# Unread loads, products, transpositions and copies ahead of a cached-attention decode kernel

## The chip, the core and the metric

The kernel runs on one core of a Trainium2 chip. The metric is device time in microseconds (us). The core has a matrix engine (PE, whose weight loads are listed as PEld), a vector engine (DVE), a scalar engine (ACT), GpSimd (POOL) and SyncE (SP), whose queue issues nearly all transfers here, and 16 DMA engines that move data between HBM and the on-chip memory of 128 partitions.

## The reference

One decode step of a transformer block with adaptive layer norm, all in float32:

```
mod = (silu(c) @ w_mod) -> sa, ca, ga, sb, cb, gb
h = layernorm(x) * (1 + ca) + sa
q = h @ wq                                  # 8 batches, 32 heads, Dh = 128
k, v = the last 2048 of 8192 cached rows of each of 8 batches x 8 KV heads
x = x + ga * (softmax(q k^T / sqrt(128)) v) @ wo
h = layernorm(x) * (1 + cb) + sb
x = x + gb * (relu(h @ w1 + b1)**2 @ w2 + b2)
```

The part of the caches that is read is 64 MiB of K and 64 MiB of V, each float32. The cache lies as (batch, KV head, row, 128): one head is 4 MiB apart from the next, one batch 32 MiB.

## The kernel before

The kernel is one long stream of 1 to 2 MiB transfers on SP's queue into eight buffers, `slot0` to `slot7`, of 128 partitions x 16 KiB. The list `loads` fixes their order: `w_mod` for the first modulation (`modA`), two pieces of `wq`, then K and V blocks with the other weights between them, `V` five blocks behind `K` (`V_LAG`). `pump()` issues the next load whenever a slot is free, and `done()` frees a slot after its last reader. A block (`load`, L96) is one KV head of two batches: each batch is 1 MiB, contiguous in HBM, and goes to every second partition (`t[u::2, :]`).

The work ahead of the first block is short: SP issues `w_mod`, while ACT and DVE build `cT`, the transposed silu of the condition (L208 to L211, L204); PE makes the modulation from both (L220); a layer norm; and the first half of q (L266). Then a loop over 32 blocks transposes each K block on PE with a multiplication by the identity (L299), copies the result out of PSUM on ACT and DVE in turn (L300), multiplies by q (L311), and, with a softmax per KV head, multiplies V (L391). [...] Products with 32 weight columns are issued in fours, one for each quarter of the array, and overlap. The output projection and the MLP end the kernel.

The order on each engine is the order in which the code is written (`manual_schedule`); waits are generated from reads and writes of tiles. The pools `work`, `ktp` and the four PSUM pools are opened at the start; the slots lie in `consts`.

Of the kernel before, what the change touches and what calls it, by code (L numbers as in the profile page):

```python
# [8 lines left out]
F32 = mybir.dt.float32  # L9
# [5 lines left out]
SLOTS = 8  # L15
# [5 lines left out]
def tile_adaln_cached_attention_mlp(  # L21
# [14 lines left out]
    nc = tc.nc  # L36
    P = 128
    B, HKV, SK, DH = k_cache.shape
# [3 lines left out]
    W = min(4096, max(256, SK // 4))  # L42
    F = w1.shape[1]
    NJ = 2 * W // P
# [7 lines left out]
    assert (B, D, DH, REP, NJ, NQ, F) == (8, 512, 128, 4, 32, 4, 1792)  # L52

    consts = ctx.enter_context(tc.tile_pool(name="consts", bufs=1))
    work = ctx.enter_context(tc.tile_pool(name="work", bufs=2))
    ktp = ctx.enter_context(tc.tile_pool(name="ktp", bufs=6))
    ps_kt = ctx.enter_context(tc.tile_pool(name="ps_kt", bufs=2, space=bass.MemoryType.PSUM))
    ps_m = ctx.enter_context(tc.tile_pool(name="ps_m", bufs=2, space=bass.MemoryType.PSUM))
    ps_o = ctx.enter_context(tc.tile_pool(name="ps_o", bufs=2, space=bass.MemoryType.PSUM))
    ps_1 = ctx.enter_context(tc.tile_pool(name="ps_1", bufs=1, space=bass.MemoryType.PSUM))  # L60
    ctx.enter_context(tc.manual_schedule())


# [8 lines left out]
    ident = consts.tile([P, P], F32, name="ident")  # L72
# [4 lines left out]
    nc.vector.memset(eps, EPS)  # L77


    slots = [consts.tile([P, NJ * DH], F32, name=f"slot{i}") for i in range(SLOTS)]  # L80
    free = list(range(SLOTS))
    held = {}
    r_kc = "(p kc) n -> p kc n"
# [355 lines left out]
    for s in range(N + PV_LAG + 1):  # L439
        g, i = divmod(s, C)  # L440
# [55 lines left out]
    for kc in range(NQ):  # L496
        for g in range(NQ):
# [4 lines left out]
                start=False,  # L502
                stop=(kc == NQ - 1),
# [16 lines left out]
    for f in range(FC):  # L520
        for q in range(NQ):
# [4 lines left out]
                start=False,  # L526
                stop=(f == FC - 1),
# [41 lines left out]
```

## Time and profile before

| what | value |
|---|---|
| median of the runs | 405.19 us (2 runs: 405.01 to 405.38) |
| span of the profiled execution | 403.6 us |
| around the span | 1.6 us to the median |
| PE, DVE, ACT, POOL busy | 83%, 44%, 24%, 1% |
| moved by DMA | 165.25 MB, mean 409 GB/s |

The median is that of unprofiled runs; the page shows one profiled execution, and the difference of 1.6 us is what lies around its span. "Busy" of PE is pipelined time, so 83% is not a share of its peak. The DMA rows carry the weight here: how much was moved, at what rate, and how long a transfer took from its issue to its landing.

### The profile page before, as it was taken

The page shows a single profiled execution, that of the slowest core. Times are in us where ns is not written, and L with a number is a line of the kernel's source. Part 1 is how long each engine was busy: PE and PEld are TensorE (multiplying, and loading weights), DVE is VectorE, ACT ScalarE, POOL GpSimd, SP SyncE. Part 2 cuts the span into 40 slices and gives each one's busy share as a digit, 9 for nine tenths or more (in the row PEclk, how much of TensorE's full clock was granted, in tenths as well). Part 3 has the DMA queues.
Part 4 walks back from the last instruction along what each step waited for, and adds up shares of the span by engine and source line. Part 5 has one row for each costly group of instructions (what it writes and reads, how often), then busy time and mean ns, then how long its engine had stood idle before and what let it go on. Part 6 is the DMA issues. An engine that isn't in the chain of part 4 may idle for free.

```text
span 403.6 us, 6379 instructions
## 1 busy us (share of the span) xinstructions
PE 333.1 (83%) x2632; PEld 170.0 (42%) x2632; DVE 177.2 (44%) x405; ACT 94.9 (24%) x168; POOL 4.1 (1%) x12
## 2 busy tenths in 40 slices
PE   0688899898998398999998899988688999884685
PEld 0245455354544155445544454444344454331124
DVE  5223345345554235445644464446344554344222
ACT  1223244123312022222222322232122322120000
POOL 4000000000000000000000000000000000000000
PEclk9789999999999889999999999999999999969659
DMA  8999999999999999999999999999999999999970
GB/s 312 429 430 424 418 429 429 427 423 421 433 429 412 430 430 424 428 429 418 433 425 430 424 432 420 434 416 429 429 425 430 425 425 430 421 427 426 408 304 8
DMA packets 15406, 165.25 MB, mean 409 GB/s; under 512 B 2441, under 2 KB 2705, under 8 KB 4497
## 3 DMA queue, kind: packets, MB, share of 16 engines
q1 hardware_dynamic: 15168, 164.70, 96.8%
q8 instruction: 21, 0.34, 0.3%
q10 hardware_dynamic: 144, 0.13, 0.1%
q14 instruction: 9, 0.07, 0.0%
q0 software_dynamic: 64, 0.01, 0.0%
HBM read 164.77 MB, written 0.07 MB: 408 GB/s over the span
## 4 chain that ended last, share of the span: by engine, by line
DMA 64%; PE 24%; DVE 6%; ACT 4%; issue 1%; ACTq 0%; DVEq 0%; SPq 0%
DMA slot<-in_A_v_cache_dram 25%; DMA slot<-in_A_k_cache_dram 20%; DMA slot<-in_A_wo_dram 17%; PE kt_ps L299 8%; PE s_ps L311 4%; PE o_ps L391 3%; PE m_ps L266 2%; DVE kT L300 2%; ACT kT L300 2%; DMA slot<-in_w_mod_dram 2%; PE m_ps L498 1%; PE m_ps L220 1%; PE m_ps L522 1%; DVE o_sb L404 1%; PE wo_ps L428 1%
## 5 line engine op out<-in xcount | busy, mean ns | idle before, releaser
L299 PE MATMUL kt_ps<-ident,slot 128*128 128x128 f32 x1024 | 150.2, 285 | 33.1 <-DMA slot<-in_A_k_cache_dram 14.9
L299 PEld LDWEIGHTS kt_ps<-ident,slot 128*128 128x128 f32 x1024 | 110.5, 143 | 106.2 <-issue 63.0
L300 DVE COPY kT<-kt_ps 128x512 f32<-128x512 f32 x128 | 88.3, 690 | 103.9 <-PE kt_ps L299 93.3
L300 ACT COPY kT<-kt_ps 128x512 f32<-128x512 f32 x128 | 74.9, 585 | 212.7 <-PE kt_ps L299 182.4
L391 PE MATMUL o_ps<-slot,pT 128*32 128x512 f32 x512 | 65.8, 625 | 6.4 <-DMA slot<-in_A_v_cache_dram 6.4
L311 PE MATMUL s_ps<-kT,qpad 128*32 128x512 f32 x512 | 64.3, 618 | 0.0
L404 DVE SCALAR_TENSOR_TENSOR o_sb<-o_ps,diag,o_sb 128x128 f32<-128x128 f32 x96 | 33.7, 351 | 3.4
L402 DVE TENSOR_SCALAR o_sb<-o_ps,diag 128x128 f32<-128x128 f32 x32 | 11.2, 351 | 44.5 <-PE o_ps L391 44.5
L391 PEld LDWEIGHTS o_ps<-slot,pT 128*32 128x32 f32 x512 | 16.4, 111 | 31.6 <-issue 27.5
L311 PEld LDWEIGHTS s_ps<-kT,qpad 128*32 128x32 f32 x512 | 13.3, 108 | 26.7 <-issue 26.7
L220 PE MATMUL m_ps<-slot,cT 128*32 128x256 f32 (+2 forms) x96 | 7.3, 451 | 9.1 <-DMA slot<-in_w_mod_dram 9.1
L266 PE MATMUL m_ps<-slot,h1T 128*32 128x512 f32 x64 | 9.8, 766 | 2.2 <-DVE h1T L204 2.2
L325 DVE TENSOR_REDUCE mx<-ss 128x1 f32<-128x512 f32 x8 | 5.5, 686 | 13.8 <-ACT ss L323 13.8
L413 PE MATMUL m_ps<-o_sb,pick 128*32 128x512 f32 x64 | 8.4, 594 | 3.1 <-DVE o_sb L404 1.6
L371 DVE TENSOR_TENSOR pT<-m_ps,mine 128x512 f32<-128x512 f32 x16 | 10.3, 682 | 0.4 <-PE m_ps L368 0.4
L428 PE MATMUL wo_ps<-slot,oT 128*32 128x512 f32 x64 | 9.6, 675 | 1.1 <-DVE oT L418 1.1
L417 DVE STREAM_TRANSPOSE tr<-m_ps 128x512 f32<-128x512 f32 x8 | 5.7, 716 | 9.5 <-PE m_ps L413 9.5
L220 PEld LDWEIGHTS m_ps<-slot,cT 128*32 128x32 f32 x96 | 4.4, 132 | 12.2 <-DVE cT L204 9.1
L368 PE MATMUL m_ps<-ident,pr 128*128 128x128 f32 x64 | 9.2, 292 | 0.3 <-DVE pr L352 0.3
L323 ACT COPY ss<-s_ps 128x512 f32<-128x512 f32 x8 | 4.7, 587 | 18.5 <-PE s_ps L311 18.5
L368 PEld LDWEIGHTS m_ps<-ident,pr 128*128 128x128 f32 x64 | 7.9, 151 | 1.3 <-DVE pr L352 1.3
L351 ACT ACTIVATE pr<-ss,nm 128x512 f32<-128x512 f32 x8 | 6.1, 762 | 9.5 <-DVE nm L347 9.5
(103 smaller groups left out, 91.1 us busy)
## 6 DMA issues: line engine op xcount, KB each, us to landing
slot<-in_A_k_cache_dram SPq DMA_DIRECT2D x64, 1024.0 KB, 20.0
slot<-in_A_v_cache_dram SPq DMA_DIRECT2D x64, 1024.0 KB, 19.9
slot<-in_A_wq_dram SPq DMA_DIRECT2D x4, 2048.0 KB, 19.9
slot<-in_A_wo_dram SPq DMA_DIRECT2D x4, 2048.0 KB, 22.3
slot<-in_B_w_dram SPq DMA_DIRECT2D x2, 1792.0 KB, 22.3
slot<-in_w_mod_dram SPq DMA_DIRECT2D x2, 1536.0 KB, 21.5
slot<-in_B_w_dram SPq DMA_DIRECT2D x3, 1024.0 KB, 23.5
slot<-in_w_mod_dram SPq DMA_DIRECT2D x1, 2048.0 KB, 8.2
```

The lines of the kernel that those rows point to most:

```text
L220: nc.tensor.matmul(pm[32 * q : 32 * q + 32, : nq * P].rearrange("p (m n) -> p m n", m=nq), cT[:, kc, :], wv[:, :, q, :], start=(kc == 0), ...
L266: nc.tensor.matmul(pq[32 * g : 32 * g + 32, :], hT[:, kc, :], w[:, kc % 2, 512 * g : 512 * g + 512], start=(kc == 0), stop=(kc == NQ - 1),)
L299: nc.tensor.transpose(p[:, i, :], k[:, 8 * g + 4 * a + i, :], ident)
L300: (nc.vector.tensor_copy if a else nc.scalar.copy)(t[:, 4 * a : 4 * a + 4, :], p)
L311: nc.tensor.matmul(s_ps[0][32 * g : 32 * g + 32, :].rearrange("p (i r) -> p i r", i=8), qpad[:, hk, 2 * c + u, :], KTS[n, g][:, :, u::2], ...
L368: nc.tensor.transpose(pp[:, i * P : (i + 1) * P], pr[:, 4 * a + i].rearrange("p r u -> p (r u)"), ident)
L371: nc.vector.tensor_mul(PT_[hk][:, a].rearrange("p x i r -> p i x r"), pp.rearrange("p (i x r) -> p i x r", i=4, r=2 * REP), mine.rearrange ...
L391: nc.tensor.matmul(o[32 * g : 32 * g + 32].rearrange("p j d -> p (j d)"), PT_[hk][:, h, C * g + c].rearrange("p i r -> p (i r)"), v[:, j : ...
L402: nc.vector.tensor_scalar(d, o[:, 0, :], diag[:, 0:1], None, op0=ALU.mult)
L404: nc.vector.scalar_tensor_tensor(d, o[:, j, :], diag[:, j : j + 1], d, op0=ALU.mult, op1=ALU.add)
L413: nc.tensor.matmul(pp[32 * t : 32 * t + 32, :], pick[:, t, :], o.rearrange("p c d -> p (c d)"), start=True, stop=True)
L428: nc.tensor.matmul(wo_ps[32 * i : 32 * i + 32, :], oT[hk % 2][:, i, :], w[:, 4 * (hk % 2) + i, :], start=(hk == 0), stop=(hk == HKV - 1),)
```

## The change

Ahead of everything but the constants stands a block that works on four buffers of its own: `trial0` to `trial2` (32 KiB in each of 128 partitions, 4 MiB each) and `trial_big` (64 KiB, 8 MiB). It loads parts of K (and once V) into them in five layouts, runs products and transpositions on `trial2` into two PSUM tiles, and transpositions and copies of `trial1` into `trial0` on DVE, ACT and GpSimd. Nothing of it is read by the rest. The block's pools are closed at its end, and the pools of the old kernel are opened behind it, so they take the same memory: 160 KiB in each partition for the block, 128 KiB for the slots. The slots move from `consts` to a pool of their own. The rest is unchanged, 81 lines further down (L96 is L177, L123 is L204, L220 is L301).

```diff
+    with tc.tile_pool(name="trial", bufs=1) as trial, tc.tile_pool(
+        name="ps_trial", bufs=1, space=bass.MemoryType.PSUM
+    ) as ps_trial:
+        pr_ = [trial.tile([P, 64 * DH], F32, name=f"trial{i}") for i in range(3)]
+        big = trial.tile([P, 128 * DH], F32, name="trial_big")
...
+        t0 = (SK - W) * DH
...
+        hs, bs, run = SK * DH, HKV * SK * DH, 64 * DH
+        for t, q in ((pr_[0], 0), (pr_[1], 1)):
+            nc.sync.dma_start(t, dram(k_cache, t0 + q * run, [[hs, 16], [4 * run, 8], [1, run]]))
+        for t, h in ((pr_[2], 0), (pr_[0], 1)):
+            nc.sync.dma_start(t, dram(k_cache, t0 + h * hs, [[run, 32], [bs, 4], [1, run]]))
+        for t, h in ((pr_[1], 2), (pr_[2], 3)):
+            for b in (0, 2, 1, 3):
+                nc.sync.dma_start(
+                    t[32 * b : 32 * b + 32, :], dram(k_cache, t0 + h * hs + b * bs, [[run, 32], [1, run]])
+                )
+        nc.sync.dma_start(big, dram(k_cache, t0, [[2 * run, 16], [bs, 8], [1, 2 * run]]))
+        nc.sync.dma_start(pr_[0], dram(k_cache, t0, [[bs, 8], [2 * run, 16], [1, run]]))
+        nc.sync.dma_start(pr_[1], dram(v_cache, t0, [[run, 32], [hs, 4], [1, run]]))
...
+        def product(n, dims, reps, step=32, width=512):
+            for k in range(reps):
+                for g in range(4):
+                    nc.tensor.matmul(
+                        po[n][32 * g : 32 * g + 32, :width],
+                        ident[:, 32 * (k % 4) : 32 * (k % 4) + 32],
+                        view(t, step * g, dims),
+                        start=True,
+                        stop=True,
+                    )
+
+        product(0, [[1, 512]], 12)
+        product(1, [[1, 512]], 4)
+        product(0, [[128, 64], [1, 8]], 4)
+        product(1, [[128, 64], [4, 8]], 4, step=1)
+        product(0, [[4, 8], [128, 64]], 4, step=1)
+        product(1, [[1, 8], [128, 64]], 4)
+        product(0, [[128, 64], [8, 4], [1, 2]], 4, step=2)
+        product(1, [[60, 128], [1, 4]], 4)
+        product(0, [[128, 32], [1, 16]], 4)
+        product(1, [[128, 32], [2, 16]], 4, step=1)
+        product(0, [[128, 8], [2, 64]], 4, step=1)
+        product(1, [[1, 128]], 16, width=128)
+        product(0, [[4096, 2], [1, 128]], 8, width=256)
+        for k in range(8):
+            nc.tensor.transpose(po[1][:, 128 * (k % 4) : 128 * (k % 4) + 128], t[:, 128 * k : 128 * k + 128], ident)
+        for k in range(8):
+            nc.tensor.transpose(po[0][:, 128 * (k % 4) : 128 * (k % 4) + 128], view(t, k, [[32, 128]]), ident)
+        for k in range(16):
+            g = 32 * (k % 4)
+            nc.tensor.matmul(po[1][g : g + 32, :256], view(t, k, [[4, 32]]), view(t, 0, [[4096, 2], [1, 128]]), start=True, stop=True)
+        for k in range(8):
+            nc.tensor.matmul(po[0], t[:, :128], view(t, 0, [[1, 512]]), start=True, stop=True)
+        u, w = pr_[1], pr_[0]
+        for k in range(3):
+            nc.vector.transpose(u[:, 2048 * k : 2048 * k + 2048], u[:, 2048 * k : 2048 * k + 2048])
+        nc.vector.transpose(w[:, :2048], u[:, :2048])
+        nc.vector.transpose(w[:, :512], u[:, :512])
...
+        nc.vector.tensor_copy(view(w, 0, [[512, 4], [1, 512]]), view(u, 0, [[1, 4], [4, 512]]))
+        nc.scalar.copy(w[:, 2048:4096], u[:, 2048:4096])
...
+        nc.scalar.copy(po[1], u[:, 2048:2560])
+        nc.gpsimd.tensor_copy(w[:, 4096:6144], u[:, 4096:6144])
...
+    slotp = ctx.enter_context(tc.tile_pool(name="slotp", bufs=1))
+    slots = [slotp.tile([P, NJ * DH], F32, name=f"slot{i}") for i in range(SLOTS)]
```

In `dram`, a pair is [step, count] in elements, `hs` is one KV head (4 MiB), `bs` one batch (32 MiB) and `run` 32 KiB; in `view` it is [step, count] of the elements that the moving operand takes within each partition.

What SP's queue holds at its start before the change (a row is an instruction with the tile that it writes; `DMAHW0` and the like are the counters of transfers, on which it waits for one that was issued earlier):

```order
L123 DMA slot_93<-in_w_mod_dram 128x4x1024
L123 DMA slot_94<-in_A_wq_dram 128x2x2048
L123 DMA slot_95<-in_A_wq_dram 128x2x2048
L96 DMA slot_96<-in_A_k_cache_dram 64x4096 x2
L96 DMA slot_97<-in_A_k_cache_dram 64x4096 x2
```

And after it, from the fourth transfer on (`trial_81` is `trial0`, `trial_82` is `trial1`, `trial_83` is `trial2`); ahead of these rows stand three more, into the three trial buffers, without a wait:

```order
L89 DMA trial_81<-in_A_k_cache_dram 128x1x8192 [waits DMAHW1_49]
L92 DMA trial_82<-in_A_k_cache_dram 32x8192 [waits DMAHW2_49]
L92 DMA trial_82<-in_A_k_cache_dram 32x8192 x2
L92 DMA trial_82<-in_A_k_cache_dram 32x8192 [waits DMAHW0_49]
L92 DMA trial_83<-in_A_k_cache_dram 32x8192 [waits DMAHW3_49]
L92 DMA trial_83<-in_A_k_cache_dram 32x8192 x2
L92 DMA trial_83<-in_A_k_cache_dram 32x8192 [waits DMAHW4_49]
L95 DMA trial_big<-in_A_k_cache_dram 128x1x16384 [waits DMAHW5_49]
L96 DMA trial_81<-in_A_k_cache_dram 128x1x8192 [waits DMAHW6_49]
L97 DMA trial_82<-in_A_v_cache_dram 128x1x8192 [waits DMAHW7_49,DMAHW0_49]
L204 DMA slot_484<-in_w_mod_dram 128x4x1024 [waits DMAHW3_49,DMAHW2_49,DMAHW4_49,DMAHW1_49,DMAHW5_49,DVE_49,DMAHW6_49,PE_49,DMAHW7_49,Activation_49,Pool_49]
L204 DMA slot_485<-in_A_wq_dram 128x2x2048
```

The first load of the old kernel has moved behind fifteen transfers, and it waits for counters of all of them and of PE, DVE, ACT and GpSimd.

On PE, the start before the change:

```order
L220 MATMUL m_ps<-slot_93,cT 32x256 [waits DMAHW1_49,DVE_49]
L220 MATMUL m_ps<-slot_93,cT 32x256 x15
L232 MATMUL m_ps<-xsum,sel 128x1 [waits DVE_49]
L242 MATMUL m_ps<-ssq,sel 128x1 [waits PE_49,Activation_49]
L266 MATMUL m_ps<-slot_94,h1T 32x512 [waits DMAHW2_49,DVE_49]
```

And after it, the first two and the last rows of the block, the latter with what follows:

```order
L108 MATMUL ps_trial_100<-trial_83,ident 32x512 [waits DMAHW3_49,DMAHW2_49,DMAHW4_49,DMAHW1_49,Pool_49]
L108 MATMUL ps_trial_100<-trial_83,ident 32x512 x47
L108 MATMUL ps_trial_101<-trial_83,ident 32x512 x16
L108 MATMUL ps_trial_100<-trial_83,ident 32x512 x16
L108 MATMUL ps_trial_101<-trial_83,ident 32x512 x16
```

```order
L108 MATMUL ps_trial_101<-trial_83,ident 32x128 x64
L108 MATMUL ps_trial_100<-trial_83,ident 32x256 x32
L130 MATMUL ps_trial_101<-ident,trial_83 128x128 x8
L132 MATMUL ps_trial_100<-ident,trial_83 128x128 x8
L135 MATMUL ps_trial_101<-trial_83 32x256 x16
L137 MATMUL ps_trial_100<-trial_83 128x512 x8
L301 MATMUL m_ps<-slot_484,cT 32x256 [waits DMAHW0_49,DMAHW5_49,DVE_49,DMAHW6_49,PE_49,DMAHW7_49,Activation_49,Pool_49]
L301 MATMUL m_ps<-slot_484,cT 32x256 x15
```

The block's 344 matmuls stand ahead of the modulation; their only wait is that of the first one, for the four transfers of L92 into `trial2`.

More of the change, by code (lines that the diff above doesn't have):

```diff
@@ L54, in tile_adaln_cached_attention_mlp @@
     consts = ctx.enter_context(tc.tile_pool(name="consts", bufs=1))
[L55 to L60, printed above, removed]
     ctx.enter_context(tc.manual_schedule())
@@ L77, in tile_adaln_cached_attention_mlp, with dram, view @@
     nc.vector.memset(eps, EPS)
-    slots = [consts.tile([P, NJ * DH], F32, name=f"slot{i}") for i in range(SLOTS)]
+    with tc.tile_pool(name="trial", bufs=1) as trial, tc.tile_pool(
[3 more added lines that the diff above has]
+        big = trial.tile([P, 128 * DH], F32, name="trial_big")
+        kx = k_cache.rearrange("b h s d -> (b h) (s d)")
+        t0 = (SK - W) * DH
+        def dram(src, offset, dims):
+            return bass.AP(tensor=src.tensor, offset=src.offset + offset, ap=dims)
+        hs, bs, run = SK * DH, HKV * SK * DH, 64 * DH
[11 more added lines that the diff above has]
+        nc.sync.dma_start(pr_[1], dram(v_cache, t0, [[run, 32], [hs, 4], [1, run]]))
+        po = [ps_trial.tile([P, 512], F32, name=f"ps_trial{i}") for i in range(2)]
+        t = pr_[2]
+        def view(t, offset, dims):
+            return bass.AP(tensor=t.tensor, offset=t.offset + offset, ap=[t.ap[0]] + dims)
+        def product(n, dims, reps, step=32, width=512):
[35 more added lines that the diff above has]
+        nc.vector.transpose(w[:, :512], u[:, :512])
+        nc.vector.transpose(view(w, 0, [[8, 64], [512, 4], [1, 8]]), view(u, 0, [[128, 64], [1, 32]]))
+        nc.vector.transpose(view(w, 0, [[2, 64], [128, 32]]), view(u, 0, [[128, 64], [1, 32]]))
+        nc.vector.tensor_copy(view(w, 0, [[512, 4], [1, 512]]), view(u, 0, [[1, 4], [4, 512]]))
+        nc.scalar.copy(w[:, 2048:4096], u[:, 2048:4096])
+        nc.scalar.copy(view(w, 2048, [[512, 4], [1, 512]]), view(u, 2048, [[1, 4], [4, 512]]))
+        nc.scalar.copy(view(w, 2048, [[8, 64], [512, 4], [1, 8]]), view(u, 2048, [[32, 64], [8, 4], [1, 8]]))
+        nc.scalar.copy(po[1], u[:, 2048:2560])
+        nc.gpsimd.tensor_copy(w[:, 4096:6144], u[:, 4096:6144])
+        nc.gpsimd.tensor_copy(view(w, 4096, [[512, 4], [1, 512]]), view(u, 4096, [[1, 4], [4, 512]]))
+        nc.gpsimd.tensor_mul(w[:, 4096:5120], u[:, 4096:5120], u[:, 5120:6144])
@@ new lines, in tile_adaln_cached_attention_mlp @@
+    work = ctx.enter_context(tc.tile_pool(name="work", bufs=2))
+    ktp = ctx.enter_context(tc.tile_pool(name="ktp", bufs=6))
+    ps_kt = ctx.enter_context(tc.tile_pool(name="ps_kt", bufs=2, space=bass.MemoryType.PSUM))
+    ps_m = ctx.enter_context(tc.tile_pool(name="ps_m", bufs=2, space=bass.MemoryType.PSUM))
+    ps_o = ctx.enter_context(tc.tile_pool(name="ps_o", bufs=2, space=bass.MemoryType.PSUM))
+    ps_1 = ctx.enter_context(tc.tile_pool(name="ps_1", bufs=1, space=bass.MemoryType.PSUM))
```

## The prediction

> **What bounds the kernel now.** I read the page's chain first, then the DMA rows and SP's waits, then the start of the chain in order of time.
>
> ```profile
> span 403.6 us, 6379 instructions
> DMA 64%; PE 24%; DVE 6%; ACT 4%; issue 1%; ACTq 0%; DVEq 0%; SPq 0%
> GB/s 312 429 430 424 418 429 429 427 423 421 433 429 412 430 430 424 428 429 418 433 425 430 424 432 420 434 416 429 429 425 430 425 425 430 421 427 426 408 304 8
> DMA packets 15406, 165.25 MB, mean 409 GB/s; under 512 B 2441, under 2 KB 2705, under 8 KB 4497
> SPq L96 <- DMA slot<-in_A_k_cache_dram: 97.1, 49, 3.1
> ```
>
> Transfers make up 64% of the chain that ended last, and from the second to the 37th of 40 slices they run at 412 to 434 GB/s without a gap. SP's largest wait is for transfers (97.1 us on K), not for a free slot. So the kernel is a stream of 165.25 MB at about 429 GB/s, with a short start and tail. There is no stretch in which more bytes would be free.
>
> The start of the chain (start, duration, what), and DVE's last row before PE begins:
>
> ```profile
> 0.74 8.22 DMA slot<-in_w_mod_dram
> 9.09 3.41 PE m_ps L220 x32
> 8.21 0.40 DVE L204 STREAM_TRANSPOSE cT<-e_sb 128x128 f32<-128x128 f32 x1
> ```
>
> SP issues `w_mod` at 0.74 us, it lands at 8.96, and PE starts at 9.09; DVE's preparation is ready at 8.61, 0.35 us sooner. Everything later hangs on that first issue. This gives the frame of the sum: if the first slot load is issued at time T in place of 0.74, the rest follows as before, 403.6 - 0.74 = 402.9 us of span and the 1.6 us around it: **time = T + 404.5**. With T = 0.74 that is the old 405.2, the median.
>
> **The change, part by part.** The added block does not run beside the old kernel. By the order on SP, the `w_mod` load waits for all fifteen trial transfers and for PE, DVE, ACT and GpSimd, since the slots take the block's memory. So T is the end of the block's last engine, and what counts is the longest path through the block.
>
> *What hides there.* The old start's preparation on DVE and GpSimd moves behind their trial work. Behind T, ACT's exponential and four DVE rows remain ahead of `cT`, less than the 8.22 us for which `w_mod` is under way, so it stays hidden; without that cover it would cost 2 to 3 us.
>
> *Transfers.* One trial buffer is 128 x 8192 x 4 B = 4.194 MB. Into `trial0` to `trial2` go four whole loads (L87, L89), eight quarters (L92), and the whole loads of L96 and L97; `trial_big` counts as two: ten units, 41.9 MB. They stand in one queue, and their waits on overwritten buffers always leave two or more transfers in flight, so the queue stays fed. Rates:
>
> ```profile
> slot<-in_w_mod_dram SPq DMA_DIRECT2D x1, 2048.0 KB, 8.2
> slot<-in_A_k_cache_dram SPq DMA_DIRECT2D x64, 1024.0 KB, 20.0
> 30.00:60.00 30.00, 26.77 (x192) 15.03 (x192) 11.66 (x17) 9.79 (x17) 0.00 (x0) 1.00 1.01 424
> ```
>
> The best rate is that of the stream, 429 GB/s (424 in the window from 30 to 60 us): 9.8 us a unit. The slowest large load in the rows is the first, 2.097 MB in 8.22 us from issue to landing, 255 GB/s: 16.4 us a unit. Between these ends I choose by shape. L89, L95 and L97 have rows of 32 or 64 KiB that lie side by side in HBM across the first dimension, and go to all 128 partitions, like K's: 429. L87 and L96 step 4 or 32 MiB through the cache, and L92's quarters go to 32 neighbouring partitions; no load of the stream does either, so I take 255. That a lone load's latency is in that figure makes it a bound more than a rate.
>
> [...]
>
> PE needs only the six units up to L92: L87 2 x 16.4, L89 2 x 9.8, L92 2 x 16.4, together 85.2 us from 0.74: **PE starts at 86**. Then L95, 19.6, L96, 16.4, and L97, 9.8: the last transfer lands at 132.
>
> *PE.* Rows for its kinds of work:
>
> ```profile
> L311 PE MATMUL s_ps<-kT,qpad 128*32 128x512 f32 x512 | 64.3, 618 | 0.0
> L391 PE MATMUL o_ps<-slot,pT 128*32 128x512 f32 x512 | 65.8, 625 | 6.4 <-DMA slot<-in_A_v_cache_dram 6.4
> L522 PE MATMUL m_ps<-slot,rT 128*32 128x128 f32 x112 | 3.3, 274 | 1.1 <-DVE rT L204 1.1
> L220 PE MATMUL m_ps<-slot,cT 128*32 128x384 f32 x32 | 2.9, 486 | 0.0
> L299 PE MATMUL kt_ps<-ident,slot 128*128 128x128 f32 x1024 | 150.2, 285 | 33.1 <-DMA slot<-in_A_k_cache_dram 14.9
> 17.22 6.14 PE L266 MATMUL m_ps<-slot,h1T 128*32 128x512 f32 x32 [2.21 <-DVE h1T L204]
> 69.27 3.62 PE m_ps L266 x32
> ```
>
> One record of 512 columns in fours takes 64.3 / 512 = 0.126 us of PE, two records a product. 208 products of 512 columns: 52.3 us. 64 of 128 columns at 3.3 / 112 = 0.029 a record: 3.8. 32 and 16 of 256 columns, between 0.029 and 2.9 / 32 = 0.091, at 0.06: 5.8. 16 transpositions at 150.2 / 1024 = 0.147: 2.4. The last 8 products fill the array with 128 weight columns, so none runs beside another; a record then costs four of the overlapped ones, 0.50: 8.0. Sum 72.3. PE comes from a long idle, as at L266, whose 32 records took 6.14 us at first and 3.62 later: 2.5 more.
>
> What the access patterns cost is unknown. [...] Three products (48 matmuls, 12.1 us) take single elements 16 or 512 B apart, for which PE has no row. The nearest is DVE's:
>
> ```profile
> L204 DVE STREAM_TRANSPOSE rT<-relu 128x448 f32<-128x448 f32 x1 | 0.9, 939 | 0.0
> L204 DVE STREAM_TRANSPOSE cT<-e_sb 128x128 f32<-128x128 f32 x1 | 0.4, 401 | 0.0
> L300 DVE COPY kT<-kt_ps 128x512 f32<-128x512 f32 x128 | 88.3, 690 | 103.9 <-PE kt_ps L299 93.3
> L227 DVE COPY modC<-m_ps 128x128 f32<-128x128 f32 x1 | 0.2, 247 | 0.0
> ```
>
> The transposition reads with a wide step: from 128 to 448 elements it grows by (939 - 401) / 320 = 1.68 ns an element; the contiguous copy by (690 - 247) / 384 = 1.15. The ends are nothing and a factor of 1.5, that is 6 us; I take 6, since the step there is like this one. **PE: 72.3 + 2.5 + 6 = 81 us, from 86 to 167.**
>
> *DVE, ACT, GpSimd* wait for the last transfer, at 132. DVE has six transpositions of 2048, at 1.15 to 1.68 ns 2.6 to 3.6 us each, one of 512 and one copy: 19 to 25 us, to 157 at most. ACT's and GpSimd's copies wait for the first three of DVE's, to 143 at most.
>
> ```profile
> L300 ACT COPY kT<-kt_ps 128x512 f32<-128x512 f32 x128 | 74.9, 585 | 212.7 <-PE kt_ps L299 182.4
> L175 POOL MEMSET qpad<- 128x2048 f32 x1 | 1.8, 1801 | 0.0
> ```
>
> ACT: three copies of four times 0.585 and one of 0.585, at most 8 us; its last writes the PSUM tile that PE still uses, so it follows PE by 0.6 us at most. GpSimd has a fill of 2048 elements at 1.8 us as its only row; for two copies of that size and a product of half of it I take between 5 and 16 us: to 159. All this lies beside PE's work and costs nothing while PE ends at 167; the cover is 8 us.
>
> **Sum:** T = 167, time = 167 + 404.5 = **572 us**.
>
> **The rivals.**
>
> *All layouts at the stream's rate.* For it: every saturated slice holds 412 GB/s or more, whichever weight or block is moved. Against: no such shape is among them. PE starts at 0.74 + 58.7 = 59 and ends at 140: 545 us; with free patterns too, 539.
>
> *The loads that step through the cache collide.* If the 16 engines of L87 meet at one part of the memory because their rows lie 4 MiB apart, they take turns. At half of the lone load's rate each takes 33 us: 33 more ahead of PE, 605 us. L96 is then late too: the transfers end at 181, and DVE between 200 and 206, beside PE's 200, so that up to 6 us come on top. Against it: blocks of the stream that lie 4 or 32 MiB apart follow one another at full rate, though not side by side. [...]
>
> [...]
>
> *The block is hidden, or dropped since nothing reads it: no change, 405 us.* Its place is SP's first slot load: only if that did not wait and the block's 42 MB did not stand ahead of it in the queue would the old stream start at 0.74. It decides once T is under 9 us. The order on SP and PE shows the opposite, both transfers and products ahead.
>
> **How the numbers follow.** Chances: the forecast 0.51, full rate 0.18, colliding rows 0.16, dear reads 0.10, both of these (636 us) 0.04, no change 0.01. The range, 538 to 630, takes in full rate with free patterns and each of the longer rivals, with the figures by the ports and for L87 above; beyond it lie the last two cases and tails. A change of 2% is about what a measurement can tell here: slower 0.98, the same 0.01, faster 0.01.
>
> **What would show it.** The first slot load should be issued near 167 us, PE's first trial product begin near 86, and the page gain about 42 MB. The landing of each trial load gives its rate: L92 and L87 near 255 GB/s, the others near 429. PE's row for L108 should hold close to 68 us. The span behind the first slot load should be 402.9. I am wrong if an engine other than PE ends the block, or if a layout runs far below 255 GB/s.

## The result, and the profile after

The changed kernel takes 627.57 us (2 runs: 625.94 to 629.2) against 405.19: 1.551 times as long, 95% interval 1.539 to 1.563. That lies inside the stated range, 538 to 630, and 56 us above the predicted 572. The span of the profiled execution is 624.2 us; that run is the shorter one, with 1.7 us around its span.

The page after: span, chain, rate by slice (40 slices, 15.6 us each) and bytes.

```profile
span 624.2 us, 7776 instructions
DMA 41%; PE 16%; DVE 4%; ACT 2%; issue 1%; ACTq 0%; DVEq 0%; SPq 0%
GB/s 194 214 242 437 216 218 235 203 203 137 150 111 143 0 184 432 427 429 433 424 430 432 426 430 425 434 427 428 432 427 428 430 429 431 429 429 429 428 422 105
DMA packets 16794, 207.28 MB, mean 332 GB/s; under 512 B 2672, under 2 KB 2936, under 8 KB 4728
```

Before, the rate stood at 412 GB/s or more from the second slice to the 37th. Now a stretch of thirteen slices lies ahead of that stream, mostly at half its rate and lower near its end (111 to 150 GB/s), then one slice with nothing. 42.0 MB were added, as many as the code says.

The start of SP's queue (issue time, duration of the issuing, line), and what SP waited for last ahead of L204:

```profile
0.74 1.32 SPq L87 DMA_DIRECT2D trial<-in_A_k_cache_dram  x2
2.11 23.02 SPq L89 DMA_DIRECT2D trial<-in_A_k_cache_dram  x2
44.51 20.44 SPq L92 DMA_DIRECT2D trial<-in_A_k_cache_dram  x8
69.74 0.56 SPq L95 DMA_DIRECT2D trial_big<-in_A_k_cache_dram  x1
84.52 0.57 SPq L97 DMA_DIRECT2D trial<-in_A_v_cache_dram  x1
225.21 0.58 SPq L204 DMA_DIRECT2D slot<-in_w_mod_dram  x1
SPq L204 <- ACT ps_trial L149: 5.1, 1, 5.1
```

The first slot load is issued at 225.21 us, so T, which the prediction put at 167, is 225.2. It waited last for ACT's copy of L149, not for PE. The block's engines in order of time:

```profile
104.40 68.61 PE L108 MATMUL ps_trial<-trial,ident 128*32 128x512 f32 x606 [104.40 <-DMA trial<-in_A_k_cache_dram]
178.64 1.01 PE L108 MATMUL ps_trial<-trial,ident 128*32 128x256 f32 x2 [5.63 <-issue]
185.70 7.13 PE L137 MATMUL ps_trial<-trial 128*128 128x512 f32 x16
201.20 6.70 DVE L140 STREAM_TRANSPOSE trial<-trial 128x2048 f32<-128x2048 f32 x3 [200.33 <-DMA trial<-in_A_v_cache_dram]
213.22 3.71 DVE L144 STREAM_TRANSPOSE trial<-trial 128x2048 f32<-128x2048 f32 x1
216.96 3.01 DVE L145 COPY trial<-trial 128x2048 f32<-128x2048 f32 x1
216.96 1.90 ACT L146 COPY trial<-trial 128x2048 f32<-128x2048 f32 x1 [14.52 <-DVE trial L144]
218.89 3.83 ACT L147 COPY trial<-trial 128x2048 f32<-128x2048 f32 x1
224.56 0.58 ACT L149 COPY ps_trial<-trial 128x512 f32<-128x512 f32 x1
```

A product stands as two records: the 8 of L137 are 16, at 0.446 us each (7.13 / 16). PE began at 104.4 and was done at 192.8, 8 us before the last transfer landed at 201.1. DVE started then and was done at 220.0; ACT ended the block at 225.1, since its first copy had waited until 216.96 for DVE's L144.

The transfers' rate by stretch (the last column, GB/s; the one ahead of it is the share of the 16 engines' time):

```profile
5.00:40.00 35.00, 0.00 (x0) 0.00 (x0) 0.00 (x0) 0.00 (x0) 0.00 (x0) 1.00 1.01 210
46.00:64.00 18.00, 0.00 (x0) 0.00 (x0) 0.00 (x0) 0.00 (x0) 0.00 (x0) 1.00 1.05 422
70.00:100.00 30.00, 0.00 (x0) 0.00 (x0) 0.00 (x0) 0.00 (x0) 0.00 (x0) 1.00 1.01 213
106.00:140.00 34.00, 34.00 (x223) 10.06 (x219) 0.00 (x0) 0.00 (x0) 0.00 (x0) 1.00 1.04 215
185.00:190.00 5.00, 5.00 (x26) 2.26 (x19) 0.00 (x0) 0.00 (x0) 0.00 (x0) 1.00 0.42 105
```

These are L87, L89, L92, L95 and the tail of L96. Three very different layouts share one rate, 210 to 215 GB/s, half of L89's 422, and L96 has half of that again, 105, with the engines busy for 0.42 of the time. In the first four stretches the engines count as busy throughout (shares of 1.01 to 1.05), so a busy DMA engine says nothing of its pace here.

The packets in the kept trace say how the quarter comes about. In L87's stretch sixteen rows of 32 KiB are under way at a time and each takes about 2.5 us, against sixteen at 1.2 us in L89's. In the last stretch only eight are under way, at up to 2.5 us each, which reads as half of the engines at half the pace.

### The profile page after: what moved, and what is told of

Its sections match the earlier page's. It is cut to its first block, busy times and chain, and to the rows that moved or that the text cites. A ratio compares the mean times of both kernels' runs of the same rounds, so it can differ in the third digit from the quotient of the medians.

```text
span 624.2 us, 7776 instructions
## 1 busy us (share of the span) xinstructions
PE 414.9 (66%) x3304; PEld 208.5 (33%) x3304; DVE 195.0 (31%) x413; ACT 102.9 (16%) x172; POOL 12.2 (2%) x15
## 4 chain that ended last, share of the span: by engine, by line
DMA 41%; PE 16%; DVE 4%; ACT 2%; issue 1%; ACTq 0%; DVEq 0%; SPq 0%
DMA slot<-in_A_k_cache_dram 19%; DMA slot<-in_A_v_cache_dram 13%; DMA slot<-in_A_wo_dram 7%; PE kt_ps L380 5%; PE s_ps L392 3%; PE o_ps L472 2%; DVE kT L381 2%; PE m_ps L347 1%; DMA slot<-in_w_mod_dram 1%; ACT kT L381 1%; PE m_ps L579 1%; PE m_ps L301 1%; PE m_ps L603 1%; DVE o_sb L485 0%; PE m_ps L494 0%
## 5 line engine op out<-in xcount | busy, mean ns | idle before, releaser
L108 PE MATMUL ps_trial<-trial,ident 128*32 128x512 f32 (+2 forms) x608 | 69.6, 616 | 110.0 <-DMA trial<-in_A_k_cache_dram 104.4
L108 PEld LDWEIGHTS ps_trial<-trial,ident 128*32 128x32 f32 x608 | 31.1, 115 | 147.7 <-issue 142.3
L140 DVE STREAM_TRANSPOSE trial<-trial 128x2048 f32<-128x2048 f32 x3 | 6.7, 2283 | 200.3 <-DMA trial<-in_A_v_cache_dram 200.3
L472 PE MATMUL o_ps<-slot,pT 128*32 128x512 f32 x512 | 64.1, 611 | 6.5 <-DMA slot<-in_A_v_cache_dram 5.2
L301 PE MATMUL m_ps<-slot,cT 128*32 128x256 f32 (+2 forms) x96 | 7.6, 464 | 41.0 <-DMA slot<-in_w_mod_dram 41.0
L301 PEld LDWEIGHTS m_ps<-slot,cT 128*32 128x32 f32 x96 | 4.4, 132 | 44.7 <-issue 43.8
```

The costliest lines, as they stand in the source:

```text
L108: nc.tensor.matmul(po[n][32 * g : 32 * g + 32, :width], ident[:, 32 * (k % 4) : 32 * (k % 4) + 32], view(t, step * g, dims), start=True, s ...
L301: nc.tensor.matmul(pm[32 * q : 32 * q + 32, : nq * P].rearrange("p (m n) -> p m n", m=nq), cT[:, kc, :], wv[:, :, q, :], start=(kc == 0), ...
L472: nc.tensor.matmul(o[32 * g : 32 * g + 32].rearrange("p j d -> p (j d)"), PT_[hk][:, h, C * g + c].rearrange("p i r -> p (i r)"), v[:, j : ...
```

## The experiments

All ran beside the kernel before, which took 404.0 to 405.7 us there; the times are single values. The layouts came first, then what runs behind them.

**The loads alone.** Products, transpositions and copies are cut from the block.

> The block keeps its fifteen loads alone; its products, transpositions and copies are left out. Theory A (the transfers set the block's end, and DVE and ACT come behind the last one): the loads land as after the change, the last at 201 us, the first slot load is issued there in place of 225, time 201 + 404.5 = 606 us. Theory B (the engines' work beside the loads slows them, so that the loads alone are faster): the last one lands well before 201, time below 600 us.

Measured: 601.69 us. SP's row of the first slot load:

```profile
201.24 0.58 SPq L148 DMA_DIRECT2D slot<-in_w_mod_dram  x1
```

The load is issued when the last transfer has landed, and that is at the same time as beside the products (201.1 us): theory A. The rest was 4 us shorter than its 404.5 (see the ninth run).

**Layouts apart.** The block's loads become:

```diff
+        nc.sync.dma_start(big, dram(k_cache, t0, [[2 * run, 32], [bs, 4], [1, 2 * run]]))
+        nc.sync.dma_start(pr_[0], dram(k_cache, t0, [[hs, 16], [4 * run, 8], [1, run]]))
+        nc.sync.dma_start(pr_[1], dram(k_cache, t0, [[9 * run, 16], [run, 8], [1, run]]))
+        nc.sync.dma_start(pr_[2], dram(k_cache, t0, [[hs, 32], [4 * run, 4], [1, run]]))
+        nc.sync.dma_start(pr_[0], dram(k_cache, t0, [[bs, 8], [2 * run, 16], [1, run]]))
+        for b in range(4):
+            nc.sync.dma_start(pr_[1][b::4, :], dram(k_cache, t0 + b * bs, [[run, 32], [1, run]]))
+        nc.sync.dma_start(pr_[2][:32, :], dram(k_cache, t0, [[bs, 8], [run, 4], [1, run]]))
+        nc.sync.dma_start(pr_[0], dram(v_cache, t0, [[hs, 64], [4 * run, 2], [1, run]]))
```

> The block holds loads alone, in other layouts, each on a line of its own; nothing is computed in it. In order: the 8 MiB load with first dimension 32 in place of 16 (its rows still 32 MiB apart within a group of four partitions); L87 as it is (16 x 8 rows, 4 MiB apart); 16 x 8 rows that are 288 KiB apart in place of 4 MiB; 32 x 4 rows, 4 MiB apart; L96 as it is (8 x 16 rows); four quarters on every fourth partition in place of 32 neighbours; a quarter on 32 neighbours with first dimension 8; 64 x 2 rows, 4 MiB apart. Theory P (a way into the on-chip memory, set by the partition, is shared by two engines at a time where the rows are dealt out in eights or the partitions are 32 neighbours): 20, 20, 20, 10, 40, 10, 5 us for the first seven, the eighth between 10 and 20. Theory H (rows that lie 4 or 32 MiB apart collide in HBM): 40, 20, 10, 20, 40, 10, 10 and 20 us.

A pattern's first dimension counts groups, and its second the rows of one group. Row by row they go to partitions 0 to 127 in each of the whole loads, so a group of eight fills eight neighbouring partitions; what differs from load to load is the pattern in HBM alone.

Measured: 545.37 us; the rates in the stretches of the first five loads:

```profile
5.00:20.00 15.00, 0.00 (x0) 0.00 (x0) 1.59 (x13) 0.00 (x0) 0.26 (x2) 1.00 0.98 424
25.00:43.00 18.00, 0.00 (x0) 0.00 (x0) 0.00 (x0) 0.00 (x0) 0.00 (x0) 1.00 1.03 217
45.00:63.00 18.00, 0.00 (x0) 0.00 (x0) 0.00 (x0) 0.00 (x0) 0.00 (x0) 1.00 1.00 217
64.00:74.00 10.00, 0.00 (x0) 0.00 (x0) 0.00 (x0) 0.00 (x0) 0.00 (x0) 1.00 1.17 419
100.00:120.00 20.00, 0.00 (x0) 0.00 (x0) 0.00 (x0) 0.00 (x0) 0.00 (x0) 1.00 0.50 105
```

For groups of four and eight the addresses did not matter here, the grouping did. Groups of eight rows run at 217 GB/s whether the groups lie 4 MiB or 288 KiB apart; groups of four run at 419 though they lie 4 MiB apart, and at 424 with rows of 64 KiB that step 32 MiB within a group. Groups of sixteen run at 105; they were tried at L96's own addresses only. Theory P has all five, theory H misses three of them (the first, the third and the fourth). The last three loads overlapped with L96's shape and with one another, so this run does not give them one by one.

**Groups of four in the whole block.**

```diff
-            nc.sync.dma_start(t, dram(k_cache, t0 + q * run, [[hs, 16], [4 * run, 8], [1, run]]))
+            nc.sync.dma_start(t, dram(k_cache, t0 + q * run, [[hs, 32], [4 * run, 4], [1, run]]))
-        nc.sync.dma_start(big, dram(k_cache, t0, [[2 * run, 16], [bs, 8], [1, 2 * run]]))
-        nc.sync.dma_start(pr_[0], dram(k_cache, t0, [[bs, 8], [2 * run, 16], [1, run]]))
+        nc.sync.dma_start(big, dram(k_cache, t0, [[2 * run, 32], [bs, 4], [1, 2 * run]]))
+        nc.sync.dma_start(pr_[0], dram(k_cache, t0, [[hs, 32], [2 * run, 4], [1, run]]))
```

> The whole block, with the same bytes and buffers; L87, L95 and L96 take 32 groups of four rows in place of 16 groups of eight and 8 of sixteen. L87's rows stay 4 MiB apart. Theory P: all three run at about 427 GB/s; the loads of L92 land at 80 us, the last one at 119, PE ends the block at 80 + 88 = 168 (163 if its pause of 5.6 us at 173 us after the change came from the slow transfers), time 568 to 573 us. Theory H: L87 and L96 keep their rates, L95 is faster at most by 20 us: PE starts at 104 as after the change, time 605 to 627 us.

Measured: 565.99 us. L87 and L89; L92; L95 to L97:

```profile
10.00:40.00 30.00, 0.00 (x0) 0.00 (x0) 0.00 (x0) 0.00 (x0) 0.00 (x0) 1.00 1.01 429
46.00:80.00 34.00, 0.00 (x0) 0.00 (x0) 0.00 (x0) 0.00 (x0) 0.00 (x0) 1.00 1.00 216
86.00:120.00 34.00, 34.00 (x228) 10.85 (x224) 0.00 (x0) 0.00 (x0) 0.00 (x0) 1.00 0.97 416
84.57 67.61 PE L108 MATMUL ps_trial<-trial,ident 128*32 128x512 f32 x608 [84.57 <-DMA trial<-in_A_k_cache_dram]
163.19 0.57 SPq L204 DMA_DIRECT2D slot<-in_w_mod_dram  x1
```

62 us came from the patterns of three loads, which bring as many rows to the same partitions, in groups of four. They take partly other rows for it; the layouts above show that, for L87's kind, the grouping and not the address makes the rate (217 GB/s in eights, 419 in fours, both 4 MiB apart). The time lies 2 us below theory P's band. Now PE ends the block: from 84.6 to 163.1, 78.5 us. Its pause of 5.6 us is gone.

**Without the products.**

> The whole block without its 344 products and transpositions on PE. Theory A (PE's 88 us lie beside the transfers): no difference from the kernel after the change that can be measured, 625 to 630 us, first slot load at 225. The rival, on which the prediction's sum rested (PE ends the block): at least 15 us less.

Measured: 624.81 us, with the first slot load here:

```profile
226.33 0.58 SPq L171 DMA_DIRECT2D slot<-in_w_mod_dram  x1
```

PE's 88 us cost nothing in the changed kernel: the prediction had the wrong engine at the block's end.

**ACT's copies apart from DVE's range.**

```diff
-        nc.scalar.copy(w[:, 2048:4096], u[:, 2048:4096])
+        nc.scalar.copy(w[:, 6144:8192], u[:, 2048:4096])
```

and the same offset in its two other copies to `trial0`.

> The whole block; ACT's three copies write to the last quarter of trial0 (from element 6144) in place of elements 2048 to 4095, which lie within the range that DVE's scattered transposition of L144 covers. Theory A (ACT waited for that range, and so ended the block): ACT starts behind DVE's first three transpositions, at about 208 us, and is done at 216; DVE ends the block at 220, the first slot load is issued there in place of 225, and the time falls by 5 us, to 621 to 623. The rival (ACT waits for something else, or DVE and ACT slow each other): the first slot load stays at 225.

Measured: 623.52 us, first slot load at 220.14. ACT's first copy, and SP's wait for DVE, behind which the wait of 5.1 us for ACT is gone:

```profile
205.64 1.90 ACT L146 COPY trial<-trial 128x2048 f32<-128x2048 f32 x1 [3.29 <-DVE trial L140]
SPq L204 <- DVE trial L145: 115.7, 1, 115.7
```

ACT began at 205.6 in place of 217.0. Theory A. The 5 us at the block's end were ACT's wait for L144: both write into elements 2048 to 4095, L144 every second one of them.

**Steps of PE's reads.** One load, then products alone: `product(n, [[s, 512]], 8)` for each step s.

> The block holds one load of L89's kind (4 MiB) and products of 512 columns alone, 8 rounds of four products (64 records) for each step between the elements that the moving operand takes: 1, 2, 3, 4, 5, 8, 15, 16, then pairs of neighbours 31 and 32 elements apart, then pairs 4 apart, 31 from pair to pair; ahead of them 12 contiguous rounds from a cold start. [...] Theory B (the cost grows with the step): 4 dearer than 3, 16 dearer than 5 by more than a fifth. Theory C (steps that are powers of two meet in one bank): 4, 8 and 16 dearer than 5 and 15.

Measured: 557.94 us. PE's stretches, from start to start of the next step (64 records each), for steps 1, 2, 3, 4, 5 and 16, and pairs 32 apart:

```profile
25.22:32.08 6.86, 6.86 (x68) 2.13 (x64) 1.00 0.00 0
32.08:39.32 7.24, 7.24 (x69) 2.10 (x65) 1.00 0.01 2
39.32:50.14 10.82, 10.82 (x68) 2.21 (x64) 1.00 0.00 0
50.14:64.59 14.45, 14.45 (x69) 2.38 (x64) 1.00 0.00 1
64.59:79.26 14.67, 14.67 (x68) 3.14 (x64) 1.00 0.00 0
107.94:122.54 14.60, 14.60 (x69) 3.17 (x65) 1.00 0.01 1
131.79:142.75 10.96, 10.96 (x68) 3.58 (x64) 1.00 0.01 1
```

Twice the time from step 4 on (14.45 against 6.86, a factor of 2.1), flat to 16 (8 and 15 took 14.7 and 14.0), half way at 3 (10.82): B and C fall. Pairs whose two elements lie 4 apart took 14.2. Pairs of neighbours took 10.96 at 32 apart and 9.25 at 31, 1.6 and 1.35 times the contiguous reads; why they cost that is not shown here.

**Quarters on every fourth partition.**

```diff
-                    t[32 * b : 32 * b + 32, :], dram(k_cache, t0 + h * hs + b * bs, [[run, 32], [1, run]])
+                    t[b::4, :], dram(k_cache, t0 + h * hs + b * bs, [[run, 32], [1, run]])
```

> The whole block; L92's quarters go to every fourth partition in place of 32 neighbours, with the same bytes from the same places. Theory P (ways into the on-chip memory, set by the partition): the eight quarters take 20 us in place of 39, PE starts at 85, the last load lands at 181, the first slot load is issued at 205, time 605 to 608 us. The rival (a transfer to 32 partitions is slow whichever they are): no change, 625 to 630.

Measured: 606.49 us, PE from 84.6, first slot load at 204.95. The rate while the quarters ran:

```profile
66.00:84.00 18.00, 0.00 (x0) 0.00 (x0) 0.00 (x0) 0.00 (x0) 0.00 (x0) 1.00 1.16 437
```

Theory P: which 32 partitions, not how many (437 GB/s here, 213 for 32 neighbours after the change). PE paused here too, as after the change: its L108 took until 161.4, 77 us in place of 67.6. It did so in the fifth run as well.

**All loads spread.** The edits of the third and the seventh run together.

> The whole block; L87, L95 and L96 in groups of four rows as in the third run, and the quarters on every fourth partition. This is the prediction's first rival, all loads at the stream's rate, made true. Theory P: 41.9 MB at 427 GB/s, the last load at 100 to 104 us, PE from 62 to 65 and for 79 us, first slot load at 141 to 144, time 541 to 547 us. If the two edits do not add up, above 550.

Measured: 547.16 us, PE from 64.4 to 144.6, first slot load at 144.70. The edits add up (0.2 us above the expected band, with T 0.7 above its own), and the prediction's first rival, 545 us, was priced rightly for loads like these.

**The kernel before, a second profile.**

> The kernel before, unchanged, for a second profile of it. In all seven profiles with the block that came ahead of this one, the part behind the first slot load took 396.4 to 401.6 us, where the prediction put 402.9 from the one profile of before. Theory A (that profile was at the long end of what the part takes): the span is 397 to 402.5 us. Theory B (the block makes the rest shorter): the span is again 403 to 404.5.

Measured: span 402.0 us, 403.81 us. Within theory A's band, at its edge: two profiles of before leave 401.3 and 402.9 us behind the first load, ten of the other kernels 396.4 to 401.6. That part varies by several us from one profile to the next. Whether the block also shortens it a little is not settled.

**Runs of neighbours.**

> As the run with the steps, with runs of neighbours: pairs at steps of 4, 8, 16, 24, 28, 30 and 32 elements, then runs of four at 32, 60 and 64, 8 rounds (64 records) each. [...] Theory D (a step of 128 B is special): 7 to 7.6 up to 30, about 11 at 32. Theory E (pairs grow dearer with the step): a rise from 4 to 32. [...]

Measured: 508.94 us. PE's stretches of 64 records, for pairs at steps 4, 24, 30 and 32 and runs of four at 60 and 64:

```profile
26.54:33.77 7.23, 7.23 (x68) 2.10 (x64) 1.00 0.00 0
48.46:58.69 10.23, 10.23 (x68) 2.64 (x64) 1.00 0.01 2
66.12:73.84 7.72, 7.72 (x69) 2.98 (x64) 1.00 0.01 2
73.84:84.82 10.98, 10.98 (x68) 3.33 (x64) 1.00 0.00 0
91.70:98.57 6.87, 6.87 (x69) 3.48 (x64) 1.00 0.00 0
98.57:106.69 8.12, 8.12 (x68) 4.10 (x60) 1.00 0.01 2
```

Pairs at steps 8, 16 and 28 took 7.3 to 7.4 us, runs of four at 32 took 6.9. Neither theory fits: 24 is nearly as dear as 32, and 28 and 30 between them are not. What steps of 96 and 128 B have in common is open.

## Why the prediction was right, and where it was not

**Slower by 1.55, inside the range, and in part by luck.** The frame held: the old kernel runs as before behind T, in 399.0 us of span in place of 402.9, and the median lies 3.4 us above the span in place of 1.6. So nearly all of the 56 us by which the time passed the forecast is T, 225.2 for 167. Right were the frame and the way to T: the added block stands whole ahead of the old stream. What fills T was not: by its own signs the prediction was wrong, for an engine other than PE ended the block and one layout ran far below 255 GB/s. The time lies 2.4 us under the end of the range, whose upper part takes in the longer rivals and two figures, for the quarters and for L87, that no run shows. Measured were 4.97 us for a quarter (39.8 / 8) and 21.9 for a load of L87 (43.8 / 2), and the quarters are 7 of the 69 us below.

**Transfers, the step that failed.** The bound at the slow end, 255 GB/s from the lone load, was no bound, and choosing K's rate for rows that lie side by side and go to all 128 partitions was the wrong likeness. Term by term:

| load | put at, us | measured, us | difference |
|---|---|---|---|
| L87, two | 32.8 | 43.8 | +11.0 |
| L89, two | 19.6 | 20.1 | +0.5 |
| L92, eight quarters | 32.8 | 39.8 | +7.0 |
| L95 | 19.6 | 42.2 | +22.6 |
| L96 and L97 | 26.2 | 54.5 | +28.3 |

The sum, 69 us, moved the last landing from 132 to 201. L95 failed by likeness: put with L89 for its rows, it ran like L87, whose groups of eight it shares. L96 failed by the bound, at 105 GB/s.

**The quarters were late by the partitions that they reach.** Each took 4.97 us, where the sum had 4.1, and on every fourth partition they ran at 437 GB/s in place of 213. That L87, L95 and L96 are slow for the same reason is argued, not shown, and so are the shared ways into the memory by which theory P explains it. Shown is that the rate follows the grouping in the pattern: 419 to 429 GB/s for groups of four and 210 to 217 for eight, each at more than one spacing, and 105 for sixteen; and that in the last case half as many rows are under way.

**The rival of colliding rows** came nearer in the total (605 to 611) and had the mechanism wrong: groups 4 MiB apart ran at 429 GB/s in the third run, and L89, whose neighbouring rows lie 32 MiB apart, at 422.

**PE was sized nearly right and lost its place.** Put at 81 us from 86, it took 88.4 from 104.4, of which 5.6 are the pause, and 78.5 without it in the third run. Behind the pause the granted clock fell (0.53 from 178.6 to 185 us) and the transpositions took longer: 3.9 us for the sixteen, against 2.1 in the third run. Within it two terms erred in opposite directions: a contiguous record took 0.107 us, not 0.126, and the three scattered products took 22.9 us, 2.2 times the contiguous price, where 1.5 was taken (in the steps' run 14.5 against 6.9). That the page's row for L108, 69.6 us, lies near the 68 forecast is largely these two errors cancelling. That only these three products would cost more than contiguous reads was the author's estimate: of the other patterns the trace before shows reads of every second element (L311, 618 ns a record beside 625 for L391's contiguous ones), and pairs 24 and 32 elements apart cost 1.5 and 1.6 times as much in the tenth run.

**The cover was an assumption about order.** DVE, ACT and GpSimd were to hide beside PE with 8 us to spare. With the transfers late, they stood behind everything: 24.1 us from the last landing to T. The third run shows them hidden again once the loads come early, the fourth that PE has no part in it, and the fifth what ACT added. DVE took 18.8 of it, against 19 to 25 forecast. ACT's wait for L144 was missed: its copies were said to need only the first three transpositions.

## What to carry to other kernels

Before costing a load, write down how its pattern groups the rows, and which partitions it reaches: the row length and the bytes said nothing here, and as many rows in groups of four in place of eight ran at twice the rate (429 GB/s in the third run against 210 for L87). A lone load's issue-to-landing time did not bound the rate from below (255 GB/s by it, 210 for L87 and 105 for L96). When several engines end within some 10 us of one another in the sum, the term with the least support decides which is last, and the tail behind the others must be priced as if it were not hidden.

## What the runs showed of the hardware that was not expected

- One queue ran at about 427 GB/s, at half (210 to 217) or at a quarter of it (105), by the grouping of rows in the load's pattern and by the partitions that it reaches. The engines are reported busy at half rate as at full rate (shares of 1.00 to 1.05), and for half the time at a quarter (0.42 to 0.50).
- PE's reads of single float32 elements 16 B or more apart cost 2.0 to 2.1 times the contiguous ones at steps from 16 to 64 B. Pairs cost 1.05 to 1.12 times as much at five of the eight steps tried, 1.35 times at 124 B, and 1.5 to 1.6 times at 96 and 128 B.
- PE stood still for 5.6 us in the middle of its products, and again in the fifth run (6.0) and the seventh (4.9), each time ahead of the last landing (201.1, 201.1 and 180.9 us; after the change the rate was 105 GB/s there, from 170 to 175 us). In the third and eighth runs, with the block's transfers done at that point, it did not. In the pause after the change the trace has one packet of 16 KiB on the queue for instructions, from 175.6 to 176.9 us, and PE went on 1.7 us after its end. A wait for PE's own instructions behind slow transfers would fit; the trace does not say for which engine the packet was, and no run tried it.
